# A LayerNorm's inverse root, a moved fold and a later table load in the first stage of a spectral GLU kernel

## The chip, the cores and the metric

The kernel runs on one core of one Trainium2 chip. The metric is the time of one execution on the device in microseconds (us), lower is better; of several runs the median is given. The engines are named as the profile names them: PE (TensorE, matmuls), DVE (VectorE), ACT (ScalarE), POOL (GpSimd) and SP (SyncE, which here only issues transfers).

## What is computed

```python
def _A_ref(x, w_r, w_i):                       # x: 1 x 2048 x 640
    X = rfft2(x) * (w_r + 1j * w_i)            # spectral filter over both axes
    return irfft2(X, s=(S, D))
h  = x + _A_ref(_layernorm(x), A_w_r, A_w_i)
n  = _layernorm(h)                             # (n - mean) / sqrt(var + 1e-5)
h2 = h + ((n @ w_gate) * (n @ w_up)) @ w_down  # F = 1728
```

Everything is float32. The change touches the first LayerNorm and the start of the transform, and one helper that the second LayerNorm shares.

## The kernel before

The 2048 rows lie in 16 tiles of 128 x 640 (`X[t]`, one tile per step of the first stage). The transforms are matmuls with small tables. The stages are: normalise and transform along one axis (stage 1, lines 140 to 382), the other axis with the filter and its inverse, the last inverse transform with the second LayerNorm, and the gated linear unit, which is the longest.

**Stage 1, per tile.** Tile t is loaded by one transfer on SP's queue (`load_x`; tile 0 in two halves, one on ACT's queue). DVE or ACT find its mean and variance: either by `bn_stats` and an aggregation on DVE, or by two passes with an accumulated sum on ACT (lines 195 and 196). From the variance comes r = 1/sqrt(var + eps) in `inverse_root` (lines 201 to 210): a root on ACT, a reciprocal on DVE and one Newton step of three tiny DVE instructions (lines 207, 208, 209), which makes the result exact enough. The row data themselves are not multiplied by r. They are folded, that is added to and subtracted from their mirror image, in four pieces: `odd(t)` (line 229, on POOL or DVE, from x alone), line 234 (sums, needs the doubled mean), line 238 (a short sum of 64 columns) and line 239 (differences of 320 columns). The scale r goes into the small cosine table instead: `scale_c(t)` makes a 128 x 128 table `CR[t]` = `cct` * r, on DVE for tiles 1 to 4, on ACT for tile 0 and from tile 5. Then `s1_mm(t)` multiplies the folded columns with that table: 7 matmuls of 128 columns in fp32, which the trace counts as 14. The first four matmuls need the pieces of lines 229 and 234 alone; the last three need those of lines 238 and 239. ACT moves the results out of PSUM (`s1_main`, line 278, `s1_rest`, line 275).

**What sets the order.** The program is written out by hand: on each engine instructions run in the order in which the code emits them, and semaphore waits are put where one needs another's result (`tc.manual_schedule()`). The mean and root of the following tiles are woven in between, in groups of tiles: 0, 1, (2,3), (4,5), (6 to 9), (10,11), (12,13), (14,15). Tiles named in `FOLDS` have their odd folds done by POOL. Ahead of them stands a copy of one column:

```python
if t in FOLDS:
    nc.gpsimd.tensor_copy(small.tile([P, 1], F32, tag="hold", name="hold"), folded(t)[1][:, 383:384])
    for k in FOLDS[t]:
        odd(k, nc.gpsimd)
```

Its value is never used. It reads the last column that line 239 writes, so POOL can't start its folds before that difference is done. For tile 0 `FOLDS` names tiles 1 and 2.

The start for tile 0 in the code before (lines 355 to 358; `c0` are the five steps of `inverse_root`, `e0` the three pieces of `even(0)`: lines 234, 238, 239; `f1` are the statistics of tile 1 on ACT):

```python
e0 = [f for _, f in even(0)]
c0[0]()
for f in (e0[0], c0[1], e0[1], c0[2], c0[3], e0[2], c0[4], *f1[:-1]):
    f()
```

after which the copy, two odd folds and `scale_c(0)` follow. The table `cct` (64 KB) is loaded on ACT's queue right behind its half of tile 0 (line 160).

Of the kernel before, what the change touches and what calls it, by code (L numbers as in the profile page):

```python
# [11 lines left out]
F32 = mybir.dt.float32  # L12
F32R = mybir.dt.float32r
AF = mybir.ActivationFunctionType
OP = mybir.AluOpType

P = 128
S, D, NF, FF = 2048, 640, 321, 1728
# [25 lines left out]
def view(t, offset, dims):  # L44
    return bass.AP(tensor=t.tensor, offset=t.offset + offset, ap=[list(t.ap[0])] + [list(d) for d in dims])
# [33 lines left out]
def tile_spectral_glu(ctx: ExitStack, tc: tile.TileContext, x, wre, wim, wgu, wlast, wdown, wdlast,  # L79
# [20 lines left out]
    def bank(tag, bufs=2):  # L100
        return pools["y" if tag in ("im2", "ir2") else "a"].tile([P, 512], F32, tag=tag, name=tag, bufs=bufs)
# [55 lines left out]

    load_x(nc.sync, 0, 0, 64)
    load_x(nc.scalar, 0, 64, P)
    nc.scalar.dma_start(cct, cc)  # L160
    for t in range(1, NT):
        load_x(nc.sync, t, 0, P)
    nc.sync.dma_start(fmt, fmain)

    def moments(ts, junk=None, total=None, k=0):
        n = len(ts)
        m2 = small.tile([P, n], F32, tag="m2", name="m2")
        ve = small.tile([P, n], F32, tag="ve", name="ve")

        def statistics(ts):  # L170
            n = len(ts)
            mv = small.tile([P, n, 2], F32, tag="mv", name="mv")
            fs, late = [], None
            for i, t in enumerate(ts):
                st = small.tile([P, 2, 6], F32, tag="st", name="st")
                fs.append(lambda st=st, t=t: nc.vector.bn_stats(st[:, 0], X[t][:, 0:320]))
                if late:
                    fs.append(late)
                fs.append(lambda st=st, t=t: nc.vector.bn_stats(st[:, 1], X[t][:, 320:640]))
                late = lambda st=st, i=i: nc.vector.bn_aggr(mv[:, i], st)  # L180
            fs.append(late)
            fs.append(lambda: nc.vector.tensor_scalar(m2[:, 0:n], mv[:, :, 0], 2.0, None, op0=OP.mult))
            fs.append(lambda: nc.vector.tensor_scalar(ve[:, 0:n], mv[:, :, 1], EPS, None, op0=OP.add))
            return fs

        if junk is None:
            return m2, ve, statistics(ts)
        first = statistics(ts[:k]) if k else []
        sq = small.tile([P, n], F32, tag="sq", name="sq")
        fs = []  # L190
        if total is not None:
            fs.append(lambda: nc.vector.tensor_scalar(m2, total, 2.0 / D, None, op0=OP.mult))
        for i, t in list(enumerate(ts))[k:]:
            if total is None:
                fs.append(lambda t=t, i=i: act(junk[i], X[t], AF.Identity, scale=2.0 / D, accum_out=m2[:, i:i + 1]))
            fs.append(lambda t=t, i=i: act(junk[i], X[t], AF.Square, bias=m2[:, i:i + 1], scale=-2.0,
                                           accum_out=sq[:, i:i + 1]))
        fs.append(lambda: nc.vector.tensor_scalar(ve[:, k:n], sq[:, k:n], 0.25 / D, EPS, op0=OP.mult, op1=OP.add))
        return m2, ve, first + fs

    def inverse_root(ve, r, n):
        sd = small.tile([P, n], F32, tag="sd", name="sd")
        w = small.tile([P, n], F32, tag="w", name="w")
        return [
            lambda: act(sd, ve, AF.Sqrt),
            lambda: nc.vector.reciprocal(r, sd),
            lambda: nc.vector.scalar_tensor_tensor(w, r, -0.5, r, op0=OP.mult, op1=OP.mult),  # L207
            lambda: tt(w, w, ve, op=OP.mult),
            lambda: nc.vector.scalar_tensor_tensor(r, w, 1.5, r, op0=OP.add, op1=OP.mult),
        ]  # L210

# [2 lines left out]
    def front(ts, k):  # L214
        n = len(ts)
        r = small.tile([P, n], F32, tag="r", name="r")
        junk = [fold[:, o:o + D] for o in (NR * 1026, NR * 1026 + D)]
        m2, ve, fs = moments(ts, junk * 2 if k < n else None, k=k)
        for i, t in enumerate(ts):
            SC[t] = r[:, i:i + 1], m2[:, i:i + 1]  # L220
        return fs, inverse_root(ve, r, n)

    def folded(t):
        o = t % NR * 1026
        return fold[:, o:o + 642], fold[:, o + 642:o + 1026]

    def odd(t, engine):
        f = folded(t)[0]
        engine.tensor_tensor(view(f, 161, [[321, 2], [1, 160]]), view(XP[t], 1, [[320, 2], [1, 160]]),
                             view(XP[t], 639, [[-320, 2], [-1, 160]]), op=OP.subtract)  # L230

    def even(t):
        f, j = folded(t)
        fs = [(0.47, lambda: nc.vector.scalar_tensor_tensor(view(f, 0, [[321, 2], [1, 161]]),
                                                     view(XP[t], 0, [[320, 2], [1, 161]]), SC[t][1],
                                                     view(XP[t], 640, [[-320, 2], [-1, 161]]),
                                                     op0=OP.subtract, op1=OP.add))]
        fs.append((0.14, lambda: tt(j[:, 0:64], f[:, 128:192], f[:, 449:513], op=OP.add)))
        fs.append((0.4, lambda: tt(view(j, 64, [[1, 2], [2, 160]]), view(f, 161, [[-161, 2], [1, 160]]),
                                   view(f, 482, [[-161, 2], [1, 160]]), op=OP.subtract)))  # L240
        return fs

    PS1, CR = {}, {}
# [46 lines left out]

    warm = wk([P, P], "warm")
    nc.vector.memset(warm, 0.0)
    pw = bank("re")
    for n in range(16):
        nc.tensor.matmul(pw[:, 0:P], warm, warm, start=True, stop=True)
# [22 lines left out]
    for t in range(NT):  # L318
        if t == 1:
            nc.gpsimd.dma_start(frall, frem)  # L320
        if t >= 1:
            fs = even(t)
            if t + 1 < NT and t + 1 not in ASIDE:
                fs.insert(1, (0.4, lambda: odd(t + 1, nc.vector)))
            if t < AHEAD:
                fs.insert(1 + (t <= 2), (0.2, lambda: scale_c(t)))
            if t == 1:
                fs, (recip, w, *left) = fs[1:], dve[1][0]
                for f in (c1[4], fs[0][1], fs[1][1], recip, fs[2][1], w):
                    f()  # L330
                dve[2].insert(0, left)
            elif t == 2:
                (ww, r), = dve[2]
                for f in (fs[0][1], ww, tail[2].pop(), fs[1][1], r, fs[2][1], fs[3][1]):
                    f()
            else:
                weave(fs, dve[t], t in FOLDS)
            for f in tail[t]:
                f()
            if t < AHEAD - 1:  # L340
                s1_rest(t - 1)
                main = lambda: s1_main(t - 1, PS1[t - 1][0], 0, 4)
                for f in acts[t][:1] + post[t] + ([*acts[t][1:], main] if t < 2 else [main, *acts[t][1:]]):
                    f()
            else:
                s1_main(t - 1, PS1[t - 1][0], 0, 4)
                s1_rest(t - 1)
                for f in post[t]:
                    f()
                if t + 1 in SCALE_ON_ACT:  # L350
                    scale_c(t + 1)
                for f in acts[t]:
                    f()
        else:
            e0 = [f for _, f in even(0)]
            c0[0]()
            for f in (e0[0], c0[1], e0[1], c0[2], c0[3], e0[2], c0[4], *f1[:-1]):
                f()
        if t in FOLDS:
            nc.gpsimd.tensor_copy(small.tile([P, 1], F32, tag="hold", name="hold"), folded(t)[1][:, 383:384])  # L360
            for k in FOLDS[t]:
                odd(k, nc.gpsimd)
        if t >= 1:
            for f in stats[t]:
                f()
            if AHEAD <= t + 1 < NT and t + 1 not in SCALE_ON_ACT:
                scale_c(t + 1)
        else:
            scale_c(0)
            b2a, b2, b3a, a2, b3, a3, m, v = stats[0]  # L370
            for f in (b2a, b2, b3a, b3, a2, f1[-1], acts[0][0], c1[0], *acts[0][1:], even(1)[0][1], a3, c1[1], m, c1[2],
                      v, c1[3]):
                f()
        if t == 0:
            for f in post[0]:
                f()
        s1_mm(t)
# [367 lines left out]
    def scale_shift(ts, junk, total=None):  # L745
        n = len(ts)
        r = small.tile([P, n], F32, tag="r", name="r")
        b = small.tile([P, n], F32, tag="b", name="b")
        m2, ve, fs = moments(ts, junk, total)
        cs = inverse_root(ve, r, n)  # L750
        cs.append(lambda: nc.vector.scalar_tensor_tensor(b, m2, -0.5, r, op0=OP.mult, op1=OP.mult))
        for i, t in enumerate(ts):
            SC[t] = r[:, i:i + 1], b[:, i:i + 1]
        return fs, cs
# [770 lines left out]
```

## Time and profile before

| | us |
|---|---|
| time, median of 3 runs (lowest, highest) | 677.42 (677.13, 677.56) |
| span of the profiled execution, first to last instruction | 675.8 |
| time less span | 1.6 |
| PE busy in that span | 663.8 (98%) |
| DVE busy | 470.6 (70%) |
| POOL busy | 400.9 (59%) |
| ACT busy | 322.7 (48%) |
| share of PE in the chain that ended last | 89% |

The profile is of one execution. Its page gives the span; the time that the device measured for that one execution isn't listed apart from the three runs, so the median stands for it, and the 1.6 us are what lies around the span. In a row of the timeline the first number is the start in us from the span's start, the second the duration; behind the engine and the line stand operation, output<-input tiles and their size, and in brackets how long the engine had been idle before and what ended that. An instruction's duration begins with its issue, so rows of one engine overlap by some 0.08 us.

### The profile page before, as it was taken

To read this page: it belongs to the slowest core of one execution; us is meant where nothing else is said; L and a number is where in the kernel's file an instruction comes from. 1 tells how busy PE (TensorE), PEld (TensorE's weight loads), DVE (VectorE), ACT (ScalarE), POOL (GpSimd) and SP (SyncE) were. 2 spreads that over 40 slices of the span, in tenths; PEclk is the share of its full clock that TensorE was granted. 3 is DMA by queue.
4 is the path that set the end of the run, shared out by engine and by line. 5 is a ranking of instruction groups with operands and counts; after the bars stand their busy time and mean duration, and the time that the engine had idled before them with its cause. 6 is when DMAs were issued, how large, how long until landed. Compare 5 with 4: busy or idle time off the path is not lost.

```text
span 675.8 us, 10232 instructions
## 1 busy us (share of the span) xinstructions
PE 663.8 (98%) x3695; PEld 587.9 (87%) x3695; DVE 470.6 (70%) x967; ACT 322.7 (48%) x622; POOL 400.9 (59%) x377
## 2 busy tenths in 40 slices
PE   7999999999999999999999999999999999999997
PEld 6998888887888888888888889888888888888887
DVE  6968887787866868585857657754757575756654
ACT  6977675485524344362626236534434252524220
POOL 3103334641198887878787544189687878787610
PEclk9999999999999999999999999999999999999999
DMA  9537964602212101143242458211012121212004
GB/s 321 220 101 247 266 225 153 178 22 78 79 40 78 40 37 42 40 108 69 86 90 79 97 109 281 78 41 59 21 39 79 40 78 40 79 39 80 1 0 156
DMA packets 46648, 66.11 MB, mean 98 GB/s; under 512 B 23826, under 2 KB 26318, under 8 KB 46470
## 3 DMA queue, kind: packets, MB, share of 16 engines
q1 hardware_dynamic: 45942, 62.90, 29.7%
q0 software_dynamic: 288, 2.16, 0.8%
q8 instruction: 29, 0.48, 0.3%
q10 hardware_dynamic: 368, 0.39, 0.2%
q14 instruction: 21, 0.17, 0.1%
HBM read 54.61 MB, written 10.84 MB: 97 GB/s over the span
## 4 chain that ended last, share of the span: by engine, by line
PE 89%; DMA 4%; DVE 3%; ACT 2%; issue 1%; SPq 0%; DVEq 0%; ACTq 0%
PE e L119 49%; PE d L119 26%; PE eo L119 4%; PE y L119 2%; PE im L252 2%; PE re L119 1%; PE u L454 1%; PE im L119 1%; PE im L506 1%; DMA bits<-in_mm_dram 1%; DMA wts<-in_wim_dram 1%; DMA sfar<-s1r 1%; DMA x<-in_x_dram 1%; PE ir L506 1%; ACT s L278 0%
## 5 line engine op out<-in xcount | busy, mean ns | idle before, releaser
L119 PE MATMUL e<-xt,wst 128*128 128x512 f32 x864 | 213.2, 391 | 0.0
L119 PEld LDWEIGHTS e<-xt,wst 128*128 128x128 f32 x864 | 159.8, 188 | 30.6
L1044 DVE TENSOR_TENSOR x<-d,x 128x320 f32<-128x320 f32 x280 | 123.4, 483 | 51.6 <-PE d L119 47.5
L119 PE MATMUL d<-wd,ht 128*128 128x320 f32 x832 | 143.6, 308 | 0.0
L119 PEld LDWEIGHTS d<-wd,ht 128*128 128x128 f32 x832 | 131.1, 188 | 7.6
L958 POOL TENSOR_TENSOR wst<-raw,wst 128x1024 fp32r<-128x1024 f32 x23 | 55.4, 2409 | 67.2 <-ACT wst L957 40.2
L119 PE MATMUL e<-t,wst 128*128 128x512 f32 x360 | 94.3, 392 | 0.0
L119 PEld LDWEIGHTS e<-t,wst 128*128 128x128 f32 x360 | 66.3, 188 | 12.6
L119 PE MATMUL d<-wt,ht 128*128 128x320 f32 x360 | 69.5, 310 | 0.0
L974 POOL TENSOR_TENSOR wst<-raw,wst 128x896 fp32r<-128x896 f32 (+1 forms) x46 | 65.1, 1436 | 0.2 <-ACT wst L969 0.2
L119 PEld LDWEIGHTS d<-wt,ht 128*128 128x128 f32 x360 | 57.3, 188 | 2.3
L1060 ACT ACTIVATE ht<-e 128x512 fp32r<-128x512 f32 x44 | 26.4, 599 | 51.5 <-DVE e L1123 25.9
L1099 ACT ACTIVATE h<-e 128x512 f32<-128x512 f32 x24 | 14.3, 595 | 67.3 <-PE e L119 67.3
L1019 DVE TENSOR_TENSOR x<-d,x 128x320 f32<-128x320 f32 x62 | 27.5, 485 | 23.5 <-PE d L119 23.5
L655 ACT ACTIVATE wd<-draw 128x320 fp32r<-128x320 f32 (+1 forms) x30 | 15.7, 558 | 57.5 <-POOL draw L665 54.3
L969 ACT ACTIVATE wst<-raw 128x896 fp32r<-128x896 f32 (+1 forms) x48 | 30.2, 677 | 26.5 <-POOL raw L963 25.7
L119 PE MATMUL e<-xt,wdir 128*128 128x512 f32 x180 | 42.0, 392 | 0.4 <-DVE w L207 0.2
L119 PEld LDWEIGHTS e<-xt,wdir 128*128 128x128 f32 x180 | 33.4, 188 | 8.1 <-ACT xt L780 0.7
L1119 DVE TENSOR_TENSOR e<-e,h 128x512 f32<-128x512 f32 x24 | 16.8, 699 | 30.8 <-PE e L119 17.7
L1063 DVE TENSOR_TENSOR ht<-e,ht 128x512 fp32r<-128x512 f32 x54 | 36.9, 685 | 1.6 <-ACT ht L1060 1.3
L634 POOL TENSOR_TENSOR wd<-draw,wd 128x640 fp32r<-128x640 f32 x8 | 12.4, 1576 | 40.5 <-ACT wd L633 40.5
L535 POOL CAST qr<-bits 1x128 fp32r<-1x128 f32 x15 | 12.1, 808 | 39.8 <-DVE qr L539 39.8
(234 smaller groups left out, 1199.3 us busy)
## 6 DMA issues: line engine op xcount, KB each, us to landing
raw<-in_wgu_dram SPq DMA_DIRECT2D x24, 640.0 KB
draw<-in_wdown_dram SPq DMA_DIRECT2D x24, 320.0 KB
wts<-in_wre_dram SPq DMA_DIRECT2D x16, 322.0 KB
x<-in_x_dram SPq DMA_DIRECT2D x15, 320.5 KB
out_dram<-x SPq DMA_DIRECT2D x15, 320.0 KB
bits<-in_mm_dram SPq DMA_DIRECT2D x16, 256.0 KB
wts<-in_wim_dram SPq DMA_DIRECT2D x9, 322.0 KB
zfar<-zr SPq DMA_DIRECT2D x32, 80.0 KB
```

Of the source, the lines that this page charges most:

```text
L119: nc.tensor.matmul(o, l, r, start=start, stop=stop, skip_group_check=True)
L252: nc.tensor.matmul(o, l, c, start=n == 0, stop=n == len(ls) - 1)
L655: act(o[:, 0, a:a + n], src, AF.Copy)
L958: ptt(wa[:, 1], stage[:, 0:1024], f32(wa[:, 0]), op=OP.subtract)
L969: act(ws[:, 0, o:o + b - a], stage[:, a:b], AF.Copy)
L974: ptt(ws[:, 1, o:o + b - a], stage[:, a:b], f32(ws[:, 0, o:o + b - a]), op=OP.subtract)
L1019: tt(xv, ps[b][:, 0:320], xv, op=OP.add)
L1044: tt(xv, o, xv, op=OP.add)
L1060: act(hop[:, a, 0], src, AF.Copy)
L1063: engine.tensor_tensor(hop[:, a, 1], src, f32(hop[:, a, 0]), op=OP.subtract)
L1099: act(h0, oa, AF.Copy)
L1119: tt(ob, ob, h1, op=OP.add)
```

## The change

Five things:

- `inverse_root` starts from one ACT operation, `Abs_reciprocal_sqrt`, in place of the root on ACT and the reciprocal on DVE. The Newton step stays. Where a group's statistics come from `bn_stats` alone, ACT reads the variance itself and adds eps as a bias (a new constant tile `eps`), and the separate addition on DVE (line 183) goes; the Newton step adds eps in its second instruction. Where they come from ACT's sums alone, ACT reads those sums.
- Tile 0's difference (line 239) is done by POOL, by the new function `difference`, and tile 0's `hold` copy goes.
- `scale_c(0)` is emitted between tile 1's two passes on ACT, ahead of line 196.
- `cct` is loaded on SP's queue behind tile 1, not on ACT's behind tile 0.
- The slots of the removed steps hold an empty function, so the weaving of the rest stays.

```diff
     load_x(nc.scalar, 0, 64, P)
-    nc.scalar.dma_start(cct, cc)
-    for t in range(1, NT):
+    load_x(nc.sync, 1, 0, P)
+    nc.sync.dma_start(cct, cc)
+    for t in range(2, NT):
         load_x(nc.sync, t, 0, P)
...
+            if alone:
+                spread_of["mv"] = mv[:, :, 1]
+                fs.append(lambda: None)
+            else:
+                ve = wide()
+                fs.append(lambda: nc.vector.tensor_scalar(ve[:, 0:n], mv[:, :, 1], EPS, None, op0=OP.add))
...
+            return m2, (var, 1.0, lambda w: nc.vector.scalar_tensor_tensor(w, var, EPS, w, op0=OP.add, op1=OP.mult)), fs
...
+        times = lambda w: tt(w, w, ve, op=OP.mult)
+        return m2, ((ve, None, times) if k else (sq, 0.25 / D, times)), first + fs
...
+    def inverse_root(spread, r, n):
+        src, scale, times = spread
         w = small.tile([P, n], F32, tag="w", name="w")
+        root = AF.Abs_reciprocal_sqrt
         return [
-            lambda: act(sd, ve, AF.Sqrt),
-            lambda: nc.vector.reciprocal(r, sd),
+            lambda: act(r, src, root) if scale is None else act(r, src, root, bias=eps, scale=scale),
+            lambda: None,
             lambda: nc.vector.scalar_tensor_tensor(w, r, -0.5, r, op0=OP.mult, op1=OP.mult),
-            lambda: tt(w, w, ve, op=OP.mult),
+            lambda: times(w),
             lambda: nc.vector.scalar_tensor_tensor(r, w, 1.5, r, op0=OP.add, op1=OP.mult),
...
+    def difference(t, engine=nc.vector):
+        f, j = folded(t)
+        engine.tensor_tensor(view(j, 64, [[1, 2], [2, 160]]), view(f, 161, [[-161, 2], [1, 160]]),
+                             view(f, 482, [[-161, 2], [1, 160]]), op=OP.subtract)
...
+    eps = keep.tile([P, 1], F32, name="eps")
+    nc.vector.memset(eps, EPS)
...
-            for f in (e0[0], c0[1], e0[1], c0[2], c0[3], e0[2], c0[4], *f1[:-1]):
+            for f in (e0[0], c0[2], e0[1], f1[0], c0[3], c0[4]):
                 f()
+            difference(0, nc.gpsimd)
+            scale_c(0)
+            f1[1]()
         if t in FOLDS:
-            nc.gpsimd.tensor_copy(small.tile([P, 1], F32, tag="hold", name="hold"), folded(t)[1][:, 383:384])
+            if t:
+                nc.gpsimd.tensor_copy(small.tile([P, 1], F32, tag="hold", name="hold"), folded(t)[1][:, 383:384])
             for k in FOLDS[t]:
                 odd(k, nc.gpsimd)
...
         else:
-            scale_c(0)
             b2a, b2, b3a, a2, b3, a3, m, v = stats[0]
```

Three places in the instruction order. Line numbers are those of each program; `x_68`, `x_69`, `x_70` and `x_71` are tiles 0 to 3, `m_139` and `m_141` the doubled mean of tile 0, and a bracket names the engine or transfer queue that is waited for. DVE at tile 0, before:

```order
L182 TENSOR_SCALAR m_139<-mv 128x1 [waits DVE_49]
L183 TENSOR_SCALAR ve<-mv 128x1
L234 SCALAR_TENSOR_TENSOR fold<-x_68,m_139 128x2x161 [waits DVE_49,Pool_49]
L206 RECIPROCAL r<-sd 128x1 [waits Activation_49]
L238 TENSOR_TENSOR fold<-fold 128x64 [waits DVE_49]
L207 SCALAR_TENSOR_TENSOR w<-r 128x1 [waits DVE_49]
L208 TENSOR_TENSOR w<-w,ve 128x1 [waits DVE_49]
L239 TENSOR_TENSOR fold<-fold 128x2x160
L209 SCALAR_TENSOR_TENSOR r<-w,r 128x1 [waits DVE_49]
L176 BN_STATS st<-x_70 128x6 [waits DMAHW4_49]
```

and in the change:

```order
L188 TENSOR_SCALAR m_141<-mv 128x1 [waits DVE_49]
L255 SCALAR_TENSOR_TENSOR fold<-x_68,m_141 128x2x161 [waits DVE_49,Pool_49]
L223 SCALAR_TENSOR_TENSOR w<-r 128x1 [waits Activation_49]
L259 TENSOR_TENSOR fold<-fold 128x64 [waits DVE_49]
L200 SCALAR_TENSOR_TENSOR w<-mv,w 128x1 [waits DVE_49]
L225 SCALAR_TENSOR_TENSOR r<-w,r 128x1 [waits DVE_49]
L182 BN_STATS st<-x_70 128x6 [waits DMAHW4_49]
```

The addition, the reciprocal and the difference are gone from DVE, and the first Newton step (L223) now stands ahead of the short sum (L259). POOL after the odd fold of tile 0, before:

```order
L229 TENSOR_TENSOR fold<-x_68 128x2x160 [waits DMAHW1_49,DMAHW0_49]
L360 COPY hold<-fold 128x1 [waits DVE_49]
L229 TENSOR_TENSOR fold<-x_69 128x2x160 [waits DMAHW3_49]
L229 TENSOR_TENSOR fold<-x_70 128x2x160 [waits DMAHW4_49]
L320 DMA frt<-in_frem_dram 128x1966
```

and in the change:

```order
L245 TENSOR_TENSOR fold<-x_68 128x2x160 [waits DMAHW1_49,DMAHW0_49]
L250 TENSOR_TENSOR fold<-fold 128x2x160 [waits DVE_49]
L245 TENSOR_TENSOR fold<-x_69 128x2x160 [waits DMAHW2_49]
L245 TENSOR_TENSOR fold<-x_70 128x2x160 [waits DMAHW4_49]
L342 DMA frt<-in_frem_dram 128x1966
```

The difference (L250) has taken the copy's place. What it waits for on DVE is the fold of L255, whose output it reads; the two odd folds behind it wait for their x tiles alone. ACT at its start, before:

```order
L205 ACT_TABLE_LOAD
L205 ACTIVATE sd<-ve 128x1
L195 ACTIVATE fold,m_146<-x_69 128x640
L196 ACTIVATE fold,sq<-x_69,m_146 128x640
L267 ACTIVATE bits<-cct,r 128x128
L195 ACTIVATE fold,m_165<-x_72 128x640
L205 ACTIVATE sd<-ve 128x1
```

and in the change:

```order
L221 ACT_TABLE_LOAD
L221 ACTIVATE r<-mv,eps 128x1
L209 ACTIVATE fold,m_146<-x_69 128x640
L287 ACTIVATE bits<-cct,r 128x128
L210 ACTIVATE fold,sq<-x_69,m_146 128x640
L209 ACTIVATE fold,m_161<-x_72 128x640
L221 ACTIVATE r<-sq,eps 128x1
```

Tile 0's table (bits<-cct,r) has moved ahead of tile 1's second pass; the number of instructions is the same, and there is one table load in either program.

## Rows read from the trace of the kernel before

**Rows 1.** The page, busy time and share of the span by engine.

```profile
PE 663.8 (98%) x3695; PEld 587.9 (87%) x3695; DVE 470.6 (70%) x967; ACT 322.7 (48%) x622; POOL 400.9 (59%) x377
```

**Rows 2.** Timeline of PE in stage 1: rows that begin after idle time.

```profile
8.76 1.86 PE L252 MATMUL im<-bits,fold 128*128 128x128 f32 x14 [2.04 <-ACT bits L267]
...
11.53 1.60 PE L252 MATMUL im<-bits,fold 128*128 128x128 f32 x12 [0.91 <-DVE r L206]
...
14.08 1.83 PE L252 MATMUL im<-bits,fold 128*128 128x128 f32 x14 [0.73 <-DVE bits L269]
...
16.23 1.60 PE L252 MATMUL im<-bits,fold 128*128 128x128 f32 x12 [0.31 <-ACT rest L275]
...
28.93 3.19 PE L252 MATMUL im<-bits,fold 128*128 128x128 f32 x26 [0.55 <-DVE mv L180]
```

**Rows 3.** Windows: start:end, length, busy us (instructions) by engine, clock, DMA share, GB/s.

```profile
4.00:6.00 2.00, 2.00 (x16) 2.00 (x16) 0.88 (x2) 0.00 (x0) 0.84 (x1) 1.00 1.05 354
...
20.00:24.00 4.00, 4.00 (x36) 3.94 (x36) 4.00 (x13) 4.00 (x13) 0.80 (x2) 1.00 1.04 387
```

**Rows 4.** Timeline of DVE, tile 0.

```profile
6.04 0.21 DVE L180 BATCH_NORM_AGGREGATE mv<-st 128x2 f32<-128x12 f32 x1
6.29 0.15 DVE L182 TENSOR_SCALAR m<-mv 128x1 f32<-128x1 f32 x1
...
6.56 0.55 DVE L234 SCALAR_TENSOR_TENSOR fold<-x,m 128x322 f32<-128x322 f32 x1
7.03 0.16 DVE L206 RECIPROCAL r<-sd 128x1 f32<-128x1 f32 x1
7.14 0.23 DVE L238 TENSOR_TENSOR fold<-fold 128x64 f32<-128x64 f32 x1
7.29 0.15 DVE L207 SCALAR_TENSOR_TENSOR w<-r 128x1 f32<-128x1 f32 x1
7.47 0.16 DVE L208 TENSOR_TENSOR w<-w,ve 128x1 f32<-128x1 f32 x1
7.55 0.48 DVE L239 TENSOR_TENSOR fold<-fold 128x320 f32<-128x320 f32 x1
7.95 0.15 DVE L209 SCALAR_TENSOR_TENSOR r<-w,r 128x1 f32<-128x1 f32 x1
```

**Rows 5.** Timeline of ACT in stage 1.

```profile
7.49 0.83 ACT L196 ACTIVATE fold<-x,m 128x640 f32<-128x640 f32 x1
...
8.32 0.39 ACT L267 ACTIVATE bits<-cct,r 128x128 f32<-128x128 f32 x1
...
9.85 0.20 ACT L205 ACTIVATE sd<-ve 128x1 f32<-128x1 f32 x1 [0.30 <-DVE ve L198]
...
29.70 0.20 ACT L205 ACTIVATE sd<-ve 128x2 f32<-128x2 f32 x1 [0.40 <-DVE ve L183]
```

**Rows 6.** Timeline of POOL and DVE, 8 to 13 us.

```profile
8.10 0.18 POOL L360 COPY hold<-fold 128x1 f32<-128x1 f32 x1 [2.08 <-DVE r L209]
...
12.05 0.86 POOL L229 TENSOR_TENSOR fold<-x 128x320 f32<-128x320 f32 x1
...
12.63 0.64 DVE L234 SCALAR_TENSOR_TENSOR fold<-x,m 128x322 f32<-128x322 f32 x1
```

**Rows 7.** Timeline of POOL and DVE, 267 to 271 us (second LayerNorm).

```profile
267.15 2.84 POOL L974 TENSOR_TENSOR wst<-raw,wst 128x896 fp32r<-128x896 f32 x2
...
269.40 0.62 DVE L207 SCALAR_TENSOR_TENSOR w<-r 128x8 f32<-128x8 f32 x1
269.95 0.88 POOL L665 TENSOR_TENSOR draw<-draw 128x320 f32<-128x320 f32 x1
270.05 0.80 DVE L208 TENSOR_TENSOR w<-w,ve 128x8 f32<-128x8 f32 x1
```

**Rows 8.** Timeline of POOL and DVE near 146 us.

```profile
145.72 0.16 DVE L208 TENSOR_TENSOR w<-w,ve 128x3 f32<-128x3 f32 x1
145.77 0.76 POOL L722 TENSOR_TENSOR yt<-q 128x322 f32<-128x322 f32 x1 [1.70 <-DVE w L207]
```

More of the change, by code (lines that the diff above doesn't have):

```diff
@@ L167, in moments, with wide, statistics @@
         m2 = small.tile([P, n], F32, tag="m2", name="m2")
-        ve = small.tile([P, n], F32, tag="ve", name="ve")
-        def statistics(ts):
+        spread_of = {}
+        def wide():
+            if "ve" not in spread_of:
+                spread_of["ve"] = small.tile([P, n], F32, tag="ve", name="ve")
+            return spread_of["ve"]
+        def statistics(ts, alone):
             n = len(ts)
@@ L182, in statistics @@
             fs.append(lambda: nc.vector.tensor_scalar(m2[:, 0:n], mv[:, :, 0], 2.0, None, op0=OP.mult))
-            fs.append(lambda: nc.vector.tensor_scalar(ve[:, 0:n], mv[:, :, 1], EPS, None, op0=OP.add))
-            return fs
-        if junk is None:
-            return m2, ve, statistics(ts)
-        first = statistics(ts[:k]) if k else []
+            if alone:
[4 more added lines that the diff above has]
+                fs.append(lambda: nc.vector.tensor_scalar(ve[:, 0:n], mv[:, :, 1], EPS, None, op0=OP.add))
+            return fs
+        if junk is None or k == n:
+            fs = statistics(ts, True)
+            var = spread_of["mv"]
+            return m2, (var, 1.0, lambda w: nc.vector.scalar_tensor_tensor(w, var, EPS, w, op0=OP.add, op1=OP.mult)), fs
+        first = statistics(ts[:k], False) if k else []
         sq = small.tile([P, n], F32, tag="sq", name="sq")
+        ve = wide()
         fs = []
@@ L198, in moments @@
         fs.append(lambda: nc.vector.tensor_scalar(ve[:, k:n], sq[:, k:n], 0.25 / D, EPS, op0=OP.mult, op1=OP.add))
-        return m2, ve, first + fs
-    def inverse_root(ve, r, n):
-        sd = small.tile([P, n], F32, tag="sd", name="sd")
+        times = lambda w: tt(w, w, ve, op=OP.mult)
+        return m2, ((ve, None, times) if k else (sq, 0.25 / D, times)), first + fs
+    def inverse_root(spread, r, n):
+        src, scale, times = spread
         w = small.tile([P, n], F32, tag="w", name="w")
+        root = AF.Abs_reciprocal_sqrt
         return [
-            lambda: act(sd, ve, AF.Sqrt),
-            lambda: nc.vector.reciprocal(r, sd),
+            lambda: act(r, src, root) if scale is None else act(r, src, root, bias=eps, scale=scale),
+            lambda: None,
             lambda: nc.vector.scalar_tensor_tensor(w, r, -0.5, r, op0=OP.mult, op1=OP.mult),
-            lambda: tt(w, w, ve, op=OP.mult),
+            lambda: times(w),
             lambda: nc.vector.scalar_tensor_tensor(r, w, 1.5, r, op0=OP.add, op1=OP.mult),
@@ L217, in front @@
         junk = [fold[:, o:o + D] for o in (NR * 1026, NR * 1026 + D)]
-        m2, ve, fs = moments(ts, junk * 2 if k < n else None, k=k)
+        m2, spread, fs = moments(ts, junk * 2 if k < n else None, k=k)
         for i, t in enumerate(ts):
             SC[t] = r[:, i:i + 1], m2[:, i:i + 1]
-        return fs, inverse_root(ve, r, n)
+        return fs, inverse_root(spread, r, n)
     def folded(t):
@@ L238, in even @@
         fs.append((0.14, lambda: tt(j[:, 0:64], f[:, 128:192], f[:, 449:513], op=OP.add)))
-        fs.append((0.4, lambda: tt(view(j, 64, [[1, 2], [2, 160]]), view(f, 161, [[-161, 2], [1, 160]]),
-                                   view(f, 482, [[-161, 2], [1, 160]]), op=OP.subtract)))
+        fs.append((0.4, lambda: difference(t)))
         return fs
@@ L748, in scale_shift @@
         b = small.tile([P, n], F32, tag="b", name="b")
-        m2, ve, fs = moments(ts, junk, total)
-        cs = inverse_root(ve, r, n)
+        m2, spread, fs = moments(ts, junk, total)
+        cs = inverse_root(spread, r, n)
         cs.append(lambda: nc.vector.scalar_tensor_tensor(b, m2, -0.5, r, op0=OP.mult, op1=OP.mult))
```

## The prediction

> **What bounds the kernel now.** I read the page's table of busy time first: TensorE (PE) is busy for 663.8 of 675.8 us [rows 1], so only its idle time and the end of the run can give anything back. The timeline of PE shows where it idles in the stage that is changed [rows 2]: the first real matmul starts at 8.76, after 2.04 us without work, and then PE waits 0.91, 0.73, 0.31 and 0.55 us ahead of tiles 1, 2, 3 and 10, in all 2.50 us. After tile 10 the stage runs without a gap. The windows tell why [rows 3]: between 20 and 24 us VectorE (DVE), ScalarE (ACT) and PE are all busy for 4.00 of 4.00 us. So three engines run close together here, and a microsecond taken from one is kept only where the others follow. The granted clock is 1.00 in these windows, the level of 2.4 GHz, and nothing below changes it.
>
> **How a gain would reach the end.** The later transfers and stages start when earlier results are ready, so I carry a shift of the end of this stage to the end of the run one to one. The page's span is 675.8; the median of the runs is 677.42, and I take the 1.6 us between them as unchanged. A run can tell from no change about 0.2%, which is 1.35 us.
>
> **Tile 0 step by step, if nothing collides.** The variance is ready when the aggregation ends, 6.04 + 0.21 = 6.25 [rows 4]. The new seed reads it directly, so ACT has it by about 6.5. The fold of line 234 at 6.56 doesn't come earlier, because it waits for the doubled mean of 6.29, not for the removed addition. The first Newton step can take the slot of the removed reciprocal (7.03), the short sum of line 238 stays at 7.14, the second step takes the slot at 7.29 and the last one that at 7.47. The 0.48 us difference of line 239 no longer stands between them; it was issued at 7.55 and the last step at 7.95. So the scale r would be ready at 7.47 + 0.15 = 7.62 in place of 8.10, a gain of 0.48 on DVE. Multiplying the table now stands ahead of tile 1's second pass on ACT, so it needn't wait until 8.32 [rows 5] and starts at 7.66. PE starts 0.44 after it, as now (8.32 to 8.76), so at 8.10, 0.66 earlier. Further on each removed instruction of this size frees 0.08 us of DVE's issue time (7.47 to 7.55 [rows 4]): five reciprocals ahead of tile 10, for tiles 1, (2,3), (4,5), (6 to 9) and (10,11), and the addition for (2,3), in all 0.48. DVE would reach tile 10 0.48 + 0.48 = 0.96 earlier. PE, which gains 0.66 at tile 0 and wouldn't have to wait 0.55 at tile 10 any more [rows 2], would follow, less a little that ACT holds back at tiles 4 to 9: about 0.95.
>
> **The moved difference.** That sum leaves out the engine that takes the difference. GpSimd (POOL) needs 0.86 us for a two-input pass of this shape [rows 6]; the data is needed only by the last three matmuls of tile 0, so its own length is covered by the first matmuls. Its neighbours aren't. The row of line 234 at 12.63 lasted 0.64 and ended at 13.27, 0.36 after a POOL pass ended at 12.91 [rows 6]; undisturbed it lasts 0.55. Far smaller rows show it better: near 270 us the first Newton step on 128x8 elements took 0.62 and the second 0.80, where 0.15 is usual [rows 4, 7]. They ended at 270.02 and 270.85; POOL's passes ended at 267.15 + 2.84 = 269.99 and 269.95 + 0.88 = 270.83, so in between POOL's next pass had got in. So a DVE instruction with both inputs in SBUF is held while POOL reads, and of a chain of dependent ones **one gets through at each end of a POOL pass**. In the kernel before, a small copy (line 360, 0.18 us at 8.10) held POOL back until the difference on DVE had ended. This copy is gone for tile 0: POOL's new order is the difference, then the odd folds of tiles 1 and 2, and the last two wait only for x tiles. POOL starts about 0.07 after the fold of line 234 ends, as the copy does after line 239 (8.03 to 8.10): 7.11 + 0.07 = 7.18, and then has three passes back to back. The whole Newton chain of tile 0, all of it with two inputs in SBUF, is issued into this.
>
> Who goes first can be said in part. The short sum is issued at 7.14, 0.04 ahead of POOL; at 145.72 an instruction with a lead of 0.05 wasn't held (0.16 us), and POOL's pass was as long as usual [rows 8]. So I let the first step and the sum through. The second step comes at 7.29, when POOL has been waiting for 0.1 us; no row shows a DVE instruction that follows another one directly while POOL waits, so its price lies between nothing and one pass. I take one pass: it is held until the difference ends (about 8.07), the last step is held by the odd fold of tile 1 until 8.07 + 0.86 = 8.93, and r is ready at 8.95. The page "SBUF — State Buffer" of the Trainium skill (section "Who interferes with whom") says of this port "Issue order, not op shape, decides who blocks"; by that alone the order would be sum, POOL, second step, which is this same case, and its sum is 677.7. No row here shows such a contest of three.
>
> With r at 8.95 in place of 8.10 DVE goes on with tiles 2 and 3 0.85 later; by tile 10 the freed 0.48 has come off, so DVE reaches it 0.37 late, and PE with it. ACT is hit more at first: the table pass starts at 8.99 (PE at 9.43, 0.67 late), and only then comes tile 1's second pass (0.83 us, 7.49 to 8.32). Before, from the table pass to the next root were 9.85 - 8.32 = 1.53 us, 0.30 of them a wait that goes; so tile 1's seed is at 8.99 + 1.23 + 0.83 = 11.05 against 9.85 [rows 5]. That delay of 1.2 shows at tiles 5 to 9, whose tables ACT scales. At tile 10, where PE had to wait 0.55 anyway, and at 29.70, where ACT idled for 0.40 [rows 5], it is taken up again. DVE's 0.37 stays.
>
> **The table loaded later.** 64 KB leave the time in which tile 0 lands. At the 354 GB/s of the window 4 to 6 us [rows 3] this is 0.18 us at most, and nothing if those packets went beside the others; I take 0.10 earlier. That the table now lands after tile 1 costs nothing: it is wanted at 7.66 at the earliest, over a microsecond later. The memset for the new constant lies in the wait for tile 0. The later LayerNorm lose reciprocals too, off the path, since PE hardly waits there: nothing.
>
> **Sum:** +0.37 - 0.10 = +0.27, so 677.42 + 0.27 = **677.7 us**.
>
> **Rivals.** (a) *The second step slips in ahead of POOL.* Then only the last step is held, until the difference, begun about 7.3, ends at 8.15; r is ready at 8.17, 0.07 late. DVE at tile 10: 0.07 - 0.48 = -0.41, with the load -0.51: 676.9. For it: DVE's instructions are issued some 0.08 us before the one ahead ends. Against: POOL asked first. (b) *Slower: the short sum is held as well.* Its lead over POOL is 0.04 us, but it stands behind the first step, which ends at 7.18. If POOL reads first, sum, second step and last step wait for one pass each: 7.18 + 3 x 0.86 = 9.76, r at 9.78, DVE 1.68 late, at tile 10 1.20, less 0.10: +1.1, 678.5. It decides from the point at which three passes, not two, stand ahead of r. Against: the row at 145.72 [rows 8]. (c) *No collision counts*, because POOL starts its pass later than its copy did, after the chain has run: -0.95 - 0.10 = -1.05, 676.4. Against: the chain needs until 7.47 to be issued, 0.3 us after POOL. (d) The change doesn't do what it says: the seed takes place on ACT at the same width as the root (0.20 us), and one table load stands in the order as before, so I leave it 3 in 100, with a time near 677.4.
>
> **How the numbers follow.** Forecast 45 in 100, (a) 24, (b) 20, (c) 8, (d) 3. Each may be off by some 0.4 us, since the shifts of ACT and DVE at tiles 4 to 10 are carried by hand. The range runs from (c)'s time to that of (b): 676.5 to 678.6; the half of (c) and the upper part of (b) that lie outside, with the tails, make less than 2 in 10. Faster by over 0.2% means under 676.07: a third of (c) and the tail of (a), 6 in 100. Slower by over 0.2% means over 678.77: nearly a third of (b), the tails of the others, 10 in 100. Within 0.2%: 84.
>
> **What would show it.** Right: a second Newton step and a last step of tile 0 of 0.6 us and more, each ending just after a POOL pass; tile 0's first matmul near 9.4; ACT idle for over a microsecond ahead of the table pass; tile 10 near 29.3. Wrong: a last step that ends before 7.7 with matmuls from 8.1 (then (c)), or near 8.2 (then (a)); one near 9.7 means (b). If the end of this stage moves and the run doesn't, the carrying of the shift to the end is what failed.

## The result and the profile after

The changed kernel takes **680.24 us** (median of 5, 679.48 to 681.33) against 677.42 for the kernel before on the same chip: ratio 1.0037, 95% interval 1.0024 to 1.0049. It is 2.8 us slower, outside the range of the prediction (676.5 to 678.6) and on its unlikely side. The profiled execution took 681.33 us with a span of 679.6; it is the slowest of the five, so its rows show the loss somewhat larger than the median does. The sections below read that execution and, for the runs of the study, theirs. "Granted clock" is the share of TensorE's full clock that the profile records as granted.

PE in the first stage of the changed kernel, by the timeline (these rows answer to [rows 2]; the three rows are the first matmuls of tiles 0, 1 and 10):

```profile
9.65 2.15 PE L272 MATMUL im<-bits,fold 128*128 128x128 f32 x14 [3.25 <-ACT bits L287]
12.58 2.90 PE L272 MATMUL im<-bits,fold 128*128 128x128 f32 x12 [0.78 <-DVE bits L289]
...
31.23 1.94 PE L272 MATMUL im<-bits,fold 128*128 128x128 f32 x15 [0.48 <-DVE mv L186]
```

Tile 0 starts 0.89 us later than before and tile 10 is 2.30 late, though in between PE waits less than before: the gaps ahead of tiles 2 and 3 are gone. What is longer is the work itself: 12 matmuls of tile 1 last 2.90 us where they lasted 1.60. The windows of the same execution say why (columns as in [rows 3]):

```profile
4.00:8.00 4.00, 2.40 (x20) 2.21 (x19) 2.34 (x8) 1.01 (x3) 1.32 (x2) 1.00 1.03 315
8.00:12.00 4.00, 2.15 (x14) 1.85 (x14) 3.86 (x14) 2.77 (x7) 2.64 (x4) 0.88 1.04 387
12.00:16.00 4.00, 3.42 (x16) 3.45 (x17) 3.96 (x17) 2.80 (x10) 1.51 (x4) 0.50 1.07 418
16.00:20.00 4.00, 4.00 (x28) 3.88 (x27) 3.68 (x16) 3.89 (x12) 0.47 (x1) 0.76 1.03 399
```

Behind 3.25 us without work PE's granted clock falls to 0.50, the level of 1.2 GHz, for all of 12 to 16 us and parts of the windows beside it. It may not fall in every run: the mean granted clock of the five was 0.995 (the profiled one), 0.997, 0.999, 0.999 and 1.000. How many of the last three were spared can't be told from the mean, since the record can begin late (e12 below).

What made that idle stretch is the timeline of the other engines at tile 0 (answering to [rows 4] and [rows 5]):

```profile
5.48 0.49 DVE L182 BATCH_NORM_STATS2 st<-x 128x6 f32<-128x320 f32 x1 [4.46 <-DMA x<-in_x_dram]
...
6.64 0.29 ACT L221 ACTIVATE r<-mv,eps 128x1 f32<-128x1 f32 x1 [4.01 <-DVE mv L186]
...
7.50 0.23 DVE L259 TENSOR_TENSOR fold<-fold 128x64 f32<-128x64 f32 x1
7.54 0.79 POOL L250 TENSOR_TENSOR fold<-fold 128x320 f32<-128x320 f32 x1 [1.16 <-DVE w L223]
7.64 0.71 DVE L200 SCALAR_TENSOR_TENSOR w<-mv,w 128x1 f32<-128x1 f32 x1
8.30 1.67 POOL L245 TENSOR_TENSOR fold<-x 128x320 f32<-128x320 f32 x2
8.38 0.78 DVE L225 SCALAR_TENSOR_TENSOR r<-w,r 128x1 f32<-128x1 f32 x1
...
9.20 0.40 ACT L287 ACTIVATE bits<-cct,r 128x128 f32<-128x128 f32 x1 [1.54 <-DVE r L225]
```

The second Newton step lasts 0.71 and the last one 0.78, where 0.15 is usual. They end at 8.35 and 9.16. POOL's difference ends at 8.33; its two odd folds stand in one row of 1.67 from 8.30, so the first of them ends near 9.14, half-way. That is the forecast's case, step for step. Tile 0's statistics begin 0.36 later than in the profile of before, which is part of the 0.89. Before:

```profile
5.12 0.49 DVE L176 BATCH_NORM_STATS2 st<-x 128x6 f32<-128x320 f32 x1 [4.12 <-DMA x<-in_x_dram]
```

The first stage is only part of the loss. Counting matmuls from the first, the same matmul starts later in the changed kernel by 2.24 us at 64 us, 2.22 at 176, 3.03 at 425 and 3.81 at 671. Between 176 and 671 us only the inverse root of the second LayerNorm was edited, near 270 us, and yet 1.6 us go there, spread over the whole stretch. PE doesn't idle more in that stretch; its matmuls are longer. The groups of PE's instructions by line (instructions, busy us, mean ns of one), kernel before:

```profile
L119 PE MATMUL e<-xt,wst 128*128 128x512 f32 x864 | 213.2, 391 | 0.0
L119 PE MATMUL d<-wd,ht 128*128 128x320 f32 x832 | 143.6, 308 | 0.0
L119 PE MATMUL e<-t,wst 128*128 128x512 f32 x360 | 94.3, 392 | 0.0
```

The changed kernel:

```profile
L119 PE MATMUL e<-xt,wst 128*128 128x512 f32 x864 | 214.2, 392 | 0.0
L119 PE MATMUL d<-wd,ht 128*128 128x320 f32 x832 | 143.8, 309 | 0.0
L119 PE MATMUL e<-t,wst 128*128 128x512 f32 x360 | 94.6, 393 | 0.0
```

1.5 us more in these three groups, in single matmuls that last up to 14 ns longer. What the change did to them is in the addresses, by the layout of the built program: the new constant `eps` is 4 bytes and takes a slot of 32 in `keep`, the pool of long-lived tiles. Every tile allocated behind it starts 32 bytes further on or, among the small ones, is laid out anew: the working tiles `draw`, `h0`, `h1` and `u`, and also `wt` and one of the tiles named `t` (`t3`), which PE reads. The large tiles ahead of it (`xt`, `wst`, `wd`, `ht`) stay. So the first and the second group read tiles that haven't moved at all, and still last longer.

### The profile page after: what moved, and what is told of

Its sections match the earlier page's. It is cut to its first block, busy times and chain, and to the rows that moved or that the text cites. A ratio compares the mean times of both kernels' runs of the same rounds, so it can differ in the third digit from the quotient of the medians.

```text
span 679.6 us, 10215 instructions
## 1 busy us (share of the span) xinstructions
PE 667.7 (98%) x3695; PEld 590.9 (87%) x3695; DVE 470.7 (69%) x951; ACT 323.2 (48%) x622; POOL 401.6 (59%) x377
## 4 chain that ended last, share of the span: by engine, by line
PE 92%; DVE 3%; ACT 2%; DMA 2%; issue 1%; DVEq 0%; ACTq 0%
PE e L119 49%; PE d L119 26%; PE eo L119 4%; PE im L272 2%; PE u L479 2%; PE y L119 2%; PE re L119 2%; PE im L119 2%; PE im L531 2%; DMA bits<-in_mm_dram 1%; PE ir L531 1%; DMA x<-in_x_dram 1%; ACT s L298 0%; ACT fold L210 0%; PE y L795 0%
```

## The experiments

**The theory** behind them: three costs add up, (1) the Newton chain of the inverse root, held by POOL, (2) the clock that falls behind the idle stretch which the chain makes, (3) the working tiles moved by `eps`. The rivals: only (1) and its after-effects; the later table; a general scatter of the long stage. "Before" is the median of the runs of before that stand beside each batch. `EPS` is 1e-5, `small` a pool allocated behind the working tiles.

### The eps tile elsewhere, and a spare tile in the kernel before

```diff
# e1: the change, with
-    eps = keep.tile([P, 1], F32, name="eps")
+    eps = small.tile([P, 1], F32, tag="eps", name="eps", bufs=1)
# e2: the kernel before, with
+    spare = keep.tile([P, 1], F32, name="spare")
+    nc.vector.memset(spare, EPS)
```

> The change as it is, but its 4-byte constant eps is taken from the pool of small tiles, so that the big tiles behind it in SBUF keep the addresses they had before. Theory 1 (addresses): between 200 and 660 us TensorE fell behind by 1.5 us in the changed kernel although its instructions there are the same; the constant had moved the working tiles by 32 bytes, and that is the cause. Then this drift is gone and the time falls by about 1.5 us, to about 678.7; what is left over before (about 1.3 us) is the first stage. Rival (chance): the drift belongs to the one profiled execution or to the chip; then the time stays near 680.2 and the drift, if it is seen, has nothing to do with addresses.

> The kernel before with nothing changed but a 4-byte tile in the long-lived pool, written once and never read, which moves the same working tiles by the same 32 bytes. Theory 1 (addresses): 677.4 + 1.5 = about 678.9, with the first stage as before and the loss spread over the gated linear unit. Rival (chance): 677.4, no difference.

Measured: e1 678.57 (ratio 1.0011, 1.0002 to 1.0020), e2 679.30 (1.0026, 1.0017 to 1.0035), before 677.87. An unused tile alone costs 1.43 us. Its first stage is as before (0.23 late at 64 us), its granted clock 1.00, and PE's groups read as in the changed kernel:

```profile
L119 PE MATMUL e<-xt,wst 128*128 128x512 f32 x864 | 214.2, 392 | 0.0
L119 PE MATMUL d<-wd,ht 128*128 128x320 f32 x832 | 143.9, 309 | 0.0
L119 PE MATMUL e<-t,wst 128*128 128x512 f32 x360 | 94.6, 392 | 0.0
```

In e1 the lengthening is gone: its shift is 1.05 us at 64, 176 and 425 us alike. Its Newton chain is held as in the change (0.71, 0.78), and its clock still falls; in 9 of 11 runs the mean granted clock was 0.996 or 0.997, and the two at 1.000 took 677.94 and 677.59.

### Everything moved, and moves by 64 and 128 bytes

```diff
# e10: the kernel before, with the spare tile ahead of all others
+    spare = keep.tile([P, 1], F32, name="spare")
+    nc.vector.memset(spare, EPS)
     XP = [keep.tile([P, D + 1], F32, name=f"x{t}") for t in range(NT)]
# e8 and e11: e6 (below), with a spare tile of 64 and 128 bytes behind the large ones
+    spare = keep.tile([P, 16], F32, name="spare")     # e11: 32
+    nc.vector.memset(spare, EPS)
```

> The kernel before with an unused tile of 4 bytes ahead of all others in keep, so that every tile of SBUF, the matmuls' operands too, starts 32 bytes later and nothing moves against anything else. Theory 1 (what counts is how the working tiles stand to the stationary operands' tiles, or to one another's place before): no cost, 677.2 to 677.9, no lengthening after 180 us. Rival 1b (the places themselves count): 678.6 to 679.5, with the matmuls from 180 to 660 us longer in all by 1.2 to 1.7 us, as with the spare tile behind the others (679.3).

> As e6, with a spare tile of 64 bytes in the long-lived pool, written once and never read, which moves the same working tiles by 64 bytes where the changed kernel moved them by 32. Theory 1a (what counts is where the tiles lie within 64 bytes): no loss, the time of e6. Theory 1b (any move from the old places costs, for instance against the tiles that didn't move): 1 to 1.5 above e6.

> The version with the difference on VectorE and the table first, and an unused tile of 128 bytes in keep: the working tiles start 128 bytes later (32 bytes cost 1.4 us, 64 cost 1.0). If only moves by less than some unit of 128 bytes or under cost: 677.2 to 677.7, no lengthening. If any move from the old places costs: 678.0 to 679.0.

Measured: e10 677.54 (ratio 1.0000, 0.9991 to 1.0009); e8 678.32 and e11 678.19, 0.96 and 0.83 over e6. In e10 the working tiles have the very addresses of e2, and the loss is gone:

```profile
L119 PE MATMUL e<-xt,wst 128*128 128x512 f32 x864 | 213.2, 390 | 0.0
L119 PE MATMUL d<-wd,ht 128*128 128x320 f32 x832 | 143.6, 308 | 0.0
L119 PE MATMUL e<-t,wst 128*128 128x512 f32 x360 | 94.4, 392 | 0.0
```

So it isn't the place of the working tiles that counts but their distance from the tiles ahead of them, among them PE's operands. In e1 the small tiles lie anew and the working tiles don't move, and nothing is lost; so the small ones aren't what counts. Moving by 64 or 128 bytes seems to cost too: between 176 and 671 us PE falls behind by 1.44 us in e8's profile and by 0.92 in e11's, though by time e11 can't be told from before (1.0006, 0.9997 to 1.0015). Which pair of tiles it is, and whether some distances would be faster than the old one, wasn't tried. The Trainium skill ("SBUF — State Buffer", section "Who interferes with whom") says that "PE and ACT never wait on anyone". That isn't what these 1.4 us look like: matmuls whose own operands stay in place last longer when other tiles move, which points to the accesses of another engine or of transfers. Which of them it is no run shows.

### The clock

```diff
# e5: e1; e9: the change as it stands; both with
-    for n in range(16):
+    for n in range(24):
         nc.tensor.matmul(pw[:, 0:P], warm, warm, start=True, stop=True)
# e12: the kernel before, with range(10)
```

> The change with eps in the pool of small tiles (as e1) and 24 instead of 16 warm-up matmuls, which fill TensorE's wait for tile 0. Theory 3 (clock): in 9 of 11 runs of e1 the granted clock was 0.996 or 0.997, and its profile shows the level of 1.2 GHz from 10.1 to 13.5 us, behind an idle stretch of 2.08 us; the two runs at 1.000 took 677.6 and 677.9. If the idle stretch brings the low level, the longer warm-up takes it away: nearly all runs at 1.000 and a median of about 677.8, although the Newton step is held as long as in e1. Rival: the low level has nothing to do with the idle stretch; then the clocks and the 678.6 of e1 come back.

> The change as it stands (eps in keep, the moved difference, the later load), with 24 warm-up matmuls in place of 16. Theory (two causes that add up: working tiles 32 bytes on, and TensorE at 1.2 GHz behind its longer idle stretch): granted clock 1.00 throughout, first pass of tile 0 behind under 0.6 us of idle, and 0.6 to 1.1 us less than the change: 679.0 to 679.6, with the lengthening of the matmuls from 180 to 660 us (1.5 us) still there. Rival A (addresses alone cost, the clock nothing on top of the held chain): 680.0 to 680.4. Rival B (the clock explains nearly all): 677.9 to 678.4.

> The kernel before with 10 warm-up matmuls in place of 16: nothing else differs, so tile 0 is ready at the same 8.8 us and the Newton chain is not held; TensorE idles over 3 us ahead of it in place of 2.0. Clock theory: the granted clock falls to 0.50 for some us behind that, and the time is 678.2 to 679.0 (0.6 to 1.3 us more than before). Rival (the idle stretch or the clock cost nothing by themselves, since the first stage waits for the other engines anyway): 677.3 to 677.9.

Measured: e5 677.92 (ratio 1.0006, 0.9997 to 1.0015; before 677.60), e9 679.48 (1.0028, 1.0017 to 1.0040) and e12 679.24 (1.0023, 1.0012 to 1.0034; before 677.61). With eight more warm-up matmuls the chain is held as long and PE starts no earlier, but it idles less. e9, PE:

```profile
9.69 1.86 PE L272 MATMUL im<-bits,fold 128*128 128x128 f32 x14 [0.78 <-ACT bits L287]
12.62 1.60 PE L272 MATMUL im<-bits,fold 128*128 128x128 f32 x12 [1.07 <-DVE bits L289]
```

and its window, with the clock at 1.00:

```profile
12.00:16.00 4.00, 2.63 (x21) 2.50 (x22) 3.96 (x17) 3.97 (x14) 1.49 (x4) 1.00 1.07 414
```

Tile 1 takes 1.60 us again. By medians the change gains 0.95 us by it (2.82 over before in its own batch, 1.87 here), and keeps its lengthening after 176 us (1.70 us). In e12 nothing but the warm-up is shorter; the chain isn't held, and the first stage still slows down:

```profile
9.06 5.39 PE L252 MATMUL im<-bits,fold 128*128 128x128 f32 x26 [3.36 <-ACT bits L267]
14.29 0.39 PE L252 MATMUL ir<-bits,fold 128*128 128x128 f32 x2
```

Tiles 0 and 1 now run without a gap, and tile 2 begins 1.19 later than before. (The clock record of this execution begins only at 13.69 us, so here the durations are read, not the clock column; in five of the seven runs the mean granted clock was 0.994 to 0.997.) The miss upward, 679.24 where at most 679.0 was expected, is by the profile in one place near 428 us, where it loses 0.86 ("Left open", below).

### The held chain

```diff
# e3: e1, with POOL held until r is there
+            nc.gpsimd.tensor_copy(small.tile([P, 1], F32, tag="hold", name="hold"), SC[0][0])
             difference(0, nc.gpsimd)
# e4: e1, with the difference on DVE again and the hold copy for tile 0 too
-            for f in (e0[0], c0[2], e0[1], f1[0], c0[3], c0[4]):
+            for f in (e0[0], c0[2], e0[1], f1[0], c0[3], e0[2], c0[4]):
                 f()
-            difference(0, nc.gpsimd)
# e6: e4, with cct loaded on ACT's queue behind tile 0, as before
# e7: the kernel before, with the difference on POOL and no hold copy for tile 0
```

> The change with eps in the pool of small tiles, and a copy of tile 0's r on GpSimd ahead of the moved difference, so that GpSimd can't read SBUF while VectorE runs the Newton step. Theory 2 (held instructions): the second and the last Newton step (0.71 and 0.78 us in the changed kernel) go back to 0.15, r is ready about 1.2 us earlier, TensorE starts at about 8.4 and its clock stays at full; the time is 1 to 1.5 us below the same kernel without the copy (e1), about 677. Rival (the load): the late start comes from tile 0 landing 0.36 us later and the wait for the table; then r moves, but the time by less than 0.4 us.

> The change with eps in the pool of small tiles, the difference of tile 0 back on VectorE between the second and the last Newton step, and the copy that held GpSimd back. What is left of the change is the seed, the place of the table pass and the later load of the table. Theory 2 (held instructions): r is ready 0.1 to 0.4 us earlier than before less what the load costs, so the time is 676.8 to 677.5. Rival (the seed or the table's place costs by itself): over 678.

> As e4 (seed, table pass ahead of tile 1's second pass, difference on VectorE, copy on GpSimd), but the small table is loaded as before, on ScalarE's queue behind its half of tile 0. Theory 4 (the load costs): in all four profiles with the table on SyncE's queue tile 0's statistics began at 5.44 to 5.53, with the old place at 5.12 and 5.30; then it begins at 5.1 to 5.3 again and the time is 0.2 to 0.3 below e4, about 677.15. Rival (the prediction's): the table in the way of tile 0 costs 0 to 0.18, so that this is 0 to 0.2 slower than e4, 677.4 to 677.6.

> The kernel before with one part of the change alone: tile 0's difference on GpSimd and no copy ahead of the odd folds. Theory 2 (held instructions): root and reciprocal push all three Newton instructions behind GpSimd's start, so each waits for the end of one of the three passes and r is ready at about 9.7 instead of 8.1; TensorE starts at about 10.2, its clock falls in nearly all runs, and the time is 678.7 to 679.5. Rival (what holds them is the new seed's chain, not GpSimd): r at about 7.7 and 677.3 or less.

Measured: e3 677.85 (ratio 1.0003, 0.9994 to 1.0011), e4 677.40 (0.9995, 0.9986 to 1.0004), both beside before 677.87; e6 677.36 (0.9997, 0.9989 to 1.0006) and e7 680.25 (1.0046, 1.0034 to 1.0059), beside 677.60. In e3 the Newton steps last 0.15 and 0.16 again and PE starts at 8.44:

```profile
5.44 0.49 DVE L182 BATCH_NORM_STATS2 st<-x 128x6 f32<-128x320 f32 x1 [4.43 <-DMA x<-in_x_dram]
...
7.79 0.16 DVE L225 SCALAR_TENSOR_TENSOR r<-w,r 128x1 f32<-128x1 f32 x1
...
8.44 1.86 PE L272 MATMUL im<-bits,fold 128*128 128x128 f32 x14 [0.95 <-ACT bits L287]
```

But the collision has moved to tile 1:

```profile
8.87 1.68 POOL L245 TENSOR_TENSOR fold<-x 128x320 f32<-128x320 f32 x2
...
9.76 1.13 DVE L255 SCALAR_TENSOR_TENSOR fold<-x,m 128x322 f32<-128x322 f32 x1
...
12.15 1.83 PE L272 MATMUL im<-bits,fold 128*128 128x128 f32 x12 [1.85 <-DVE bits L289]
```

Line 255 lasts 1.13 in place of 0.54, PE idles 1.85 us ahead of tile 1, and in 4 of 11 runs the granted clock fell (0.996 to 0.997). So e3 gained 0.72 us over e1, less than expected. In e7 no part of the change is left but the move to POOL, with the old chain of reciprocal and three steps:

```profile
7.49 0.71 DVE L207 SCALAR_TENSOR_TENSOR w<-r 128x1 f32<-128x1 f32 x1
8.23 0.78 DVE L208 TENSOR_TENSOR w<-w,ve 128x1 f32<-128x1 f32 x1
9.05 0.78 DVE L209 SCALAR_TENSOR_TENSOR r<-w,r 128x1 f32<-128x1 f32 x1
...
10.32 4.88 PE L252 MATMUL im<-bits,fold 128*128 128x128 f32 x26 [2.53 <-ACT bits L267]
```

All three steps wait for one pass each, PE starts 1.56 late, the clock is 0.75 in the window from 12 to 16 us, and the kernel is 2.65 us slower with every tile at its old place. The expectation missed it by 0.75 us.

e6 keeps the seed on ACT in place of root and reciprocal, and the scaled table between tile 1's passes; its chain is undisturbed, and PE starts tiles 0 and 10 at 8.60 and 28.69, 0.16 and 0.24 us ahead of before. Its time can't be told from before's, nor can e4's. No version was shown to beat the kernel before.

## Why the prediction was wrong

The forecast was slower by 0.27 us; measured were 2.82. The collision that it described took place and cost about what it said. Two other steps failed, the clock that "nothing below changes" and the constant that was put at nothing; what they cost is worked out here. The differences of medians to the run of before beside them, from e6 up to the change:

| kernel | what is added | over before, us | step |
|---|---|---|---|
| e6 | seed on ACT, table between tile 1's passes | -0.24 | -0.24 |
| e5 | difference on POOL without hold; later table (24 warm-ups) | +0.32 | +0.56 |
| e9 | `eps` in `keep` | +1.87 | +1.55 |
| the change | 16 warm-ups: the clock falls | +2.82 | +0.95 |

The steps add up by construction. By the intervals of the ratios a row is uncertain by 0.6 us (e6, e5) to 0.85 (the change), and a step by 0.6 to 1.2. So only the step of the address stands by the times alone, and e2 measures it independently (+1.43). The others rest on the traces, read from the start of tile 0's statistics to the first matmul of tile 10, which leaves out when tile 0 lands. e6, e5 and e9:

```profile
5.33 0.50 DVE L181 BATCH_NORM_STATS2 st<-x 128x6 f32<-128x320 f32 x1 [4.31 <-DMA x<-in_x_dram]
28.69 3.19 PE L271 MATMUL im<-bits,fold 128*128 128x128 f32 x26 [0.47 <-DVE mv L185]
...
5.33 0.49 DVE L182 BATCH_NORM_STATS2 st<-x 128x6 f32<-128x320 f32 x1 [4.32 <-DMA x<-in_x_dram]
29.60 3.19 PE L272 MATMUL im<-bits,fold 128*128 128x128 f32 x26 [0.47 <-DVE mv L186]
...
5.50 0.49 DVE L182 BATCH_NORM_STATS2 st<-x 128x6 f32<-128x320 f32 x1 [4.49 <-DMA x<-in_x_dram]
29.76 3.19 PE L272 MATMUL im<-bits,fold 128*128 128x128 f32 x26 [0.47 <-DVE mv L186]
```

That is 23.81 us before, 23.36 in e6, 24.27 in e5, 24.26 in e9 and 25.75 in the change; 24.59 in e1 and 24.69 in e12. The clock is worth 1.49 there between e9 and the change, in the slowest of the change's five runs; between e5 and e1, whose clock column reads 0.76 and 0.82 in the windows from 8 to 16 us, it is worth 0.32 (0.38 by medians), and 0.88 between before and e12, whose +1.63 by medians holds the place near 428 us as well. So the clock's price is between 0.3 and 1.5 us, by the execution, and 0.95 by medians.

- **"The moved difference": right.** The short sum goes through, the second step waits for the difference and the last one for the odd fold of tile 1. By the Trainium skill's rule of issue order ("SBUF — State Buffer", section "Who interferes with whom") it was to be this case, and the trace agrees (0.71 and 0.78). Its price was about right as well: in e5 and e9, where the clock doesn't fall, tile 10 is 0.46 and 0.45 us late in the reading above, where 0.37 was forecast. That the time of e5, which has all of the change but the two costs below, agrees too (0.32 over before, where the sum said 0.27) is partly luck: the earlier landing in that sum wasn't borne out, and e5's profile loses 0.48 near 428 us, at a place where e12 loses time too without any part of the change.
- **"The granted clock is 1.00 in these windows ..., and nothing below changes it": failed.** The prediction itself had PE start 0.67 late, so idle 2.7 us in place of 2.04, and priced only the start. Measured, the clock fell to 1.2 GHz, and that costs 0.95 us by medians.
- **"The memset for the new constant lies in the wait for tile 0": failed, and is the largest term.** The instruction is hidden indeed; its tile wasn't. 4 bytes in `keep` moved the working tiles, and the matmuls after 176 us are 1.6 us longer. The term stood at nothing, with a reason for the instruction and none for the tile.
- **"I carry a shift of the end of this stage to the end of the run one to one" and "The later LayerNorm ... nothing": right, as far as the shift goes.** The 2.24 of 64 us are 2.22 at 176, and in e1, which has the shared helper too, the shift is 1.05 at 64 and at 425 us. What comes on top in the change has the cause above.
- **"64 KB leave the time in which tile 0 lands ... 0.10 earlier": not borne out, perhaps of the other sign.** Tile 0's statistics start at 5.33 to 5.53 in the six profiles with the later table (mean 5.45) and at 5.12 to 5.43 in the eight with the old order (mean 5.33). By medians, e4 against e6, the order makes no difference that can be told.
- **"Tile 0 step by step, if nothing collides": right.** e3 shows the new chain undisturbed and without the difference: r is ready at 7.79 + 0.16 = 7.95, 2.51 after the start of the statistics, where before it was 8.10 - 5.12 = 2.98. That is a gain of 0.47, and 0.48 was forecast; PE gains 0.64 in the same way, and 0.66 was forecast. The seed lasts 0.29 where 0.20 was assumed, but the first Newton step stands behind the fold of line 255 and doesn't wait for it. In e6, where the difference still stands in the chain, the gain at r is 0.2. The 0.95 forecast for tile 10 was measured nowhere without a collision; e6 gains 0.45 there.
- **The rivals.** (b) was the only slower one and held the short sum, which went through. Neither it nor the tails held the two mechanisms that decided; 10 in 100 for slower by over 0.2% was too little.

**Left open.** Two single places are seen in some executions and not in others: 0.35 us at 70 to 74 us, paid in the profiles of before, the change and e1 alone, where PE waits for a transfer of `bits` (0.49 us in before's profile), and 0.5 to 0.9 us at four matmuls near 428 us (in e1, e4 to e7 and e12; 0.1 in e3 and e8; not in before, the change, e2, e9, e10 and e11). Why some executions pay and others don't wasn't traced. They blur single profiles, and the table above within its uncertainty. Open too is which accesses meet in the lengthened matmuls.

## What to carry to other kernels

A new tile, however small, moves all that is allocated behind it: so put it last, or compare the addresses of the tiles of the longest stage, before reading a difference as the work of the edit. Price an idle stretch ahead of a bound TensorE twice, by its length and by the clock behind it, and look whether a few more warm-up matmuls close it. A tiny copy that only holds an engine back can be a part of the schedule: without it the chain of dependent two-input VectorE instructions got through here at one per GpSimd pass (0.71, 0.78 and 0.78 us in e7, in place of 0.15).

## What was unexpected

- A 4-byte tile that nothing reads costs 1.43 us of 677.87 (e2); the same shift of all tiles together costs nothing (e10: 677.54 beside 677.61).
- How long PE idled doesn't alone tell whether the clock falls: it fell behind 2.08 us without work in e1's profile and not behind 2.13 in e6's or 2.04 in before's [rows 2]. In 4 of 84 runs of before the mean granted clock was 0.997, and they took 678.60 to 678.91.
- `Abs_reciprocal_sqrt` on 128x1 with `eps` as bias takes 0.28 to 0.29 us on ACT, the root 0.20 [rows 5]. The function isn't what is slower: without the bias, on 128x4, it takes as long as the root on that shape (first row the change, second row before):

```profile
21.34 0.22 ACT L221 ACTIVATE r<-ve 128x4 f32<-128x4 f32 x1
...
18.76 0.22 ACT L205 ACTIVATE sd<-ve 128x4 f32<-128x4 f32 x1
```
